# A searched order for all five engines, exchanged for another one: gated mix of a recurrent memory transformer and full attention

## The chip, the cores and the metric

One core of a Trainium2 chip runs the whole program. The metric is the device time of one execution in microseconds (us): 1329.91 as the median of three runs of the kernel before (1328.98 to 1330.77). The engines are named as in the profile: PE (TensorE matmul), PEld (TensorE weight load), DVE (VectorE), ACT (ScalarE), POOL (GpSimd) and SP (SyncE, which issues transfers).

## What is computed

Two attention models read the same input x (2048 tokens of 576 numbers, bfloat16) and are mixed by a gate per token.

```python
g = _sigmoid((x * gate_w).sum(-1, keepdims=True))
a = _A_ref(x, A_mem0, A_Wq, A_Wk, A_Wv, A_Wo, A_seg_len)   # recurrent, 64 segments
b = _B_ref(x, B_wqkv, B_wo)                                # full attention, 32 heads of 18
return g * a + (1 - g) * b
```

Model A walks through 64 segments of 32 tokens, one after the other. A segment's 8 memory rows and 32 tokens are projected to 32 heads of 128 for q, k and v, go through a masked softmax over 40 positions and an output projection; the first 8 rows of the result are the next segment's memory. Model B is plain softmax attention of 2048 by 2048 positions, with 32 heads of 18 numbers.

## The kernel before

**Work.** Model B runs as 32 groups of four heads and 512 queries, each with 16 blocks of 128 keys. One such block is a "visit": four matmuls in parallel give scores (L1066, tiles sb of three banks and sp of one), ACT takes the exponential of both (L1075 for 1536 columns, L1079 for 512), and PE multiplies the result with the values (L1089, ob). There are 512 visits. Model A's segment is a chain over several engines: PE projects q, k and v (L1438, pvv), DVE turns them (L1479) or copies them (L661), DVE or POOL puts the pieces in place (L1525 into qk, L1502 into v_sb), PE forms scores (L1539, L1547, psh), ACT the exponential (L1557), PE sums (L1568 or L1573, pss), DVE the reciprocal (L1585, rq), PE spreads it (L1593, prb), DVE scales (L1604, et), PE multiplies with v (L1615, pso), DVE or ACT copies out (ot), PE projects (L1320, acc), DVE adds (L1347 sum, L1648 obf), PE "folds" the memory rows (L1663 and L1670, pw) and DVE writes them into the next segment's input (L1679, ht). Only then can the next segment begin. The parts of model A that don't depend on the memory are computed ahead (L1157 and L1161, pv) and held in DRAM. At the start x is transposed (L724, evicted by L661 on DVE or L659 on ACT) and projected for model B (L871, L909); at the end the attention output is projected (L1834, L1838, tile po), combined with the gate on DVE (L1849), and stored by SP (L1859).

**Tile modes of PE.** A stage uses the array whole ("full", 128 rows by 128 columns), as four column strips ("col"), four row strips ("row", only the scores of model B), two row halves ("tall") or smaller squares ("quad").

**What sets the order.** `Plan` holds 8,581 operations with their dependences and with pools of numbered buffers (`tokens`): four shared PSUM banks "pb", one triple bank "sb", two "etb", and so on. `ORDER` is a table of five strings, one for each engine. A string holds differences between the numbers of successive operations, so the five lists together give the order on every engine, and also which engine does an operation that two can do. `run` takes the heads of the five lists in turn and replays them with stored durations; the replay decides which buffer of a pool an operation gets. `FULL` lists operations that are to use their whole-array form instead of the column form. Where the replay sees PE idle for long enough, `zeros` puts in a filler: a multiplication with zeros that adds nothing (L1037 in column strips, four matmuls each; L1043 whole).

```python
            at, queues[e] = 0, []
            for step in ORDER[e].split():
                at += int(step)
                queues[e].append(self.ops[at])
```

An engine works strictly through its list: a head that waits holds up all behind it, transfers included where that engine issues them.

Of the kernel before, what the change touches and what calls it, by code (L numbers as in the profile page):

```python
# [10 lines left out]
ACT = mybir.ActivationFunctionType  # L11
# [5 lines left out]
    "PE":  # L17
        "19 15 -5 -5 188 -24 -75 -39 -14 224 -234 75 -27 -14 116 -48 6 -50 32 3 3 -101 24 -14 82 12 6 -39 -13 -10 -14 "
        "91 -42 -9 42 33 -27 -36 3 -12 54 15 -27 39 -6 -15 -3 27 -21 -12 202 -166 6 164 -161 3 162 -5 4 -152 -6 163 "
        "-154 3 -9 159 7 -151 6 -9 158 -7 -139 -6 151 5 -147 9 137 5 -145 -3 147 7 -142 -3 142 7 -122 -21 147 -5 -139 "  # L20
        "143 -137 142 -145 9 135 7 -3 -121 -15 143 -134 -3 141 -5 -130 6 128 5 -130 3 126 11 -7 2293 -2420 138 2276 7 "
        "1 1 -2286 5 2273 1 -2275 2285 1 -2281 2271 11 -2283 2284 9 -2288 2289 -2290 2283 1 1 -2280 2281 5 4 1 -4 5 "
        "-2288 -5 2205 -2201 2202 88 -87 -2198 2199 1 3 -2204 5 2206 1 1 1 -2210 5 2206 3 -13 1 13 -2211 5 2207 -13 1 "
        "17 -2213 2209 -2204 2205 -2206 2216 -6 7 1 -2213 2225 -11 12 1 -21 1 -2208 2209 -2204 -1 2212 13 1 -11 1 1 1 "
        "-2213 2260 1 -47 52 -4 5 1 -5 -2259 -5 2273 -3 4 1 1 64 -2336 11 -7 2339 2 1 -2 3 3 -1 -2334 2336 -2337 2334 "
        "-73 1 1 -2258 2259 3 1 1 10 -9 -2261 -5 4 2272 -7 1 7 1 -2269 2262 10 1 -10 11 -2275 5 2271 9 -6 1 1 -2277 5 "
        "2273 4 -2278 2279 1 -2275 2319 7 -4 -2323 2321 7 -6 -2317 2311 8 6 -1 -2325 5 2322 4 -16 14 -2325 5 2319 -14 "
        "16 -17 -2305 5 -1 2363 7 -6 1 -2360 2366 -5 1 -39 -2324 5 2363 1 1 -2366 2338 -16 -2317 2319 -2320 2322 "
        "-2317 2331 -11 -2321 2334 -12 1 1 12 -2325 -7 2335 1 1 1 2 -2329 -1 2376 -4 3 -2 1 4 2 -2375 2374 -29 27 -26 "
        "3 -2350 2353 -5 -2343 2349 -5 3 -1 6 3 -2356 2354 -2349 2352 -2 3 3 -1 21 -22 -2355 5 2374 33 1 1 -33 34 -20 "  # L30
        "21 -2412 5 2374 -2375 2411 1 1 -24 25 -2409 2386 -13 37 -36 1 1 12 -2389 5 2387 1 1 1 -2391 2393 -2388 -1 "
        "2409 4 -3 7 14 -20 1 22 -2 1 2 4 -2434 2433 -2 1 -23 10 -9 1 -2412 2422 -6 -2411 2419 -3 2 21 -25 -2 1 -2414 "
        "5 2437 33 1 -32 33 1 1 -21 -2454 5 2437 36 1 1 -24 25 1 -2478 2454 -2449 2436 1 14 -13 1 -2440 5 2450 1 1 1 "
        "-2454 2456 -2443 -9 2494 1 2 -1 2 4 -2489 2486 1 1 -2489 2460 4 -1 4 -2462 2463 -7 1 4 -1 10 2 -2473 2472 -5 "
        "-2462 2470 -1 -4 -2466 2465 -1 27 -2484 2520 1 1 -36 37 1 -22 -14 -2491 7 2500 -2501 2487 37 1 1 1 -2522 "
        "2523 -38 13 -12 1 1 -2489 2501 -2496 -1 2500 1 1 1 -2496 2498 -2501 2524 4 -3 1 1 -2520 2525 -3 10 -9 10 -9 "
        "10 -2530 -5 2529 7 1 20 -25 -2 1 -2527 2555 -2550 2531 1 20 -18 -1 -2534 2567 -31 4 -2533 2531 45 -46 32 -30 "
        "45 1 1 -15 -2567 7 2576 -32 33 1 1 -2580 5 2543 1 1 13 -2559 2547 -2542 2557 1 1 1 -2561 2563 -2552 -7 2599 "
# [1863 lines left out]
```

## Time and profile before

| | before |
|---|---|
| median of three runs | 1329.91 us |
| the profiled execution: first to last instruction | 1326.1 us |
| around it (median less span) | 3.8 us |
| PE busy | 1291.3 us, 97% |
| ACT busy | 1113.3 us, 84% |
| DVE busy | 820.1 us, 62% |
| POOL busy | 611.5 us, 46% |

The page gives the profiled execution no time of its own beside its span. PE's busy time takes in the modelled ends of pipelined matmuls, so 97% doesn't mean that 3% alone is lost: gaps of some tenths of a microsecond are covered by it. They show in the starts of successive matmuls and in the idle time ahead of PEld.

### The profile page before, as it was taken

What the parts mean: (1) busy time and instruction counts of PE and PEld (TensorE: products, weight loads), DVE (VectorE), ACT (ScalarE), POOL (GpSimd) and SP (SyncE); (2) the same over time, 40 slices, a digit from 0 to 9 for tenths busy, and PEclk for the clock granted to TensorE, in tenths of its full rate; (3) what the DMA queues carried; (4) which work ended last, traced back from release to release, by engine and by line L of the source; (5) the groups of instructions that cost most, each with busy time, mean ns of one, the idle gap of its engine ahead of it and who ended that gap; (6) DMA issues with size and microseconds to landing.
All of it is one profiled execution on the core that took longest, in us unless ns stands there. A gap on an engine that the chain in (4) does not pass through costs nothing.

```text
span 1326.1 us, 73242 instructions
## 1 busy us (share of the span) xinstructions
PE 1291.3 (97%) x32951; PEld 694.1 (52%) x32951; DVE 820.1 (62%) x1821; ACT 1113.3 (84%) x1329; POOL 611.5 (46%) x1260
## 2 busy tenths in 40 slices
PE   8999899999999999999999999999999999999998
PEld 5555454555555545555555545555554445454445
DVE  5334466666666656666665665657665666666667
ACT  3688889988978888888888888888878999898895
POOL 4552475555444454343463454554345434644330
PEclk9999999999999999999999999999999999999999
DMA  8997420011201021200210111200113010201024
GB/s 254 290 309 233 134 64 22 29 47 37 64 18 44 26 57 30 53 17 23 58 48 17 35 50 32 68 24 26 38 35 81 16 32 11 52 21 34 19 79 149
DMA packets 110073, 88.63 MB, mean 67 GB/s; under 512 B 67271, under 2 KB 100375, under 8 KB 109759
## 3 DMA queue, kind: packets, MB, share of 16 engines
q1 hardware_dynamic: 92471, 50.92, 13.7%
q0 software_dynamic: 15152, 30.83, 7.7%
q8 instruction: 258, 4.23, 1.3%
q10 hardware_dynamic: 2136, 2.19, 0.6%
q14 instruction: 56, 0.46, 0.1%
HBM read 52.74 MB, written 31.12 MB: 63 GB/s over the span
## 4 chain that ended last, share of the span: by engine, by line
PE 83%; DVE 6%; ACT 4%; issue 3%; DMA 2%; POOL 1%; SPq 0%; DVEq 0%; ACTq 0%; POOLq 0%
PE pvv L1438 30%; PE sb L1066 11%; PE acc L1320 11%; PE ob L1089 8%; PE pv L1157 5%; ACT etb L1075 3%; PE pso L1615 3%; PE pq L871 3%; PE pv L1161 2%; PE psh L1547 2%; DVE v_sb L1502 2%; PE po L1834 1%; PE prb L1593 1%; PE pvb L909 1%; PE psh L1539 1%
## 5 line engine op out<-in xcount | busy, mean ns | idle before, releaser
L1075 ACT ACTIVATE etb<-sb 128x1536 bf16<-128x1536 f32 x512 | 743.4, 1452 | 121.5 <-PE sp L1066 83.0
L1079 ACT ACTIVATE etb<-sp 128x512 bf16<-128x512 f32 x512 | 305.2, 596 | 0.1
L1502 POOL COPY v_sb<-tm 32x512 bf16<-32x512 bf16 x344 | 217.1, 631 | 174.2 <-DVE tm L661 117.0
L1479 DVE STREAM_TRANSPOSE tf<-pvv 128x512 f32<-128x512 f32 x256 | 181.2, 714 | 171.0 <-PE pvv L1438 164.0
L1438 PEld LDWEIGHTS <-ht 128*32 128x32 bf16 (+1 forms) x7680 | 171.6, 94 | 218.6 <-issue 119.3
L1525 POOL CAST qk<-tf 128x512 bf16<-128x512 f32 x130 | 81.4, 628 | 297.3 <-DVE tf L1479 295.3
L1066 PE MATMUL sb<-qch,kch 32*128 32x512 bf16 x1536 | 200.6, 384 | 2.7 <-ACT etb L1075 1.2
L1089 PE MATMUL ob<-etb,vch 128*32 128x512 bf16 x2048 | 202.6, 382 | 0.3 <-DVE tq L1117 0.3
L1066 PE MATMUL sp<-qch,kch 32*128 32x512 bf16 x512 | 196.1, 383 | 0.1
L1438 PE MATMUL pvv<-wk_m,ht 128*32 128x512 bf16 x2048 | 165.0, 381 | 0.3
L1438 PE MATMUL pvv<-wq_m,ht 128*32 128x512 bf16 x2048 | 163.2, 381 | 1.3 <-DVE ht L1679 0.5
L1320 PE MATMUL acc<-wo,ot 128*32 128x288 bf16 (+1 forms) x6144 | 161.5, 247 | 1.5 <-DVE ot L661 0.5
L1438 PE MATMUL pvv<-wv_m,ht 128*32 128x512 bf16 x2048 | 154.6, 381 | 0.0
L1320 PEld LDWEIGHTS <-ot 128*32 128x32 bf16 x6144 | 112.4, 96 | 32.8 <-issue 10.7
L661 DVE CAST ot<-pso 128x320 bf16<-128x320 f32 x193 | 88.0, 484 | 49.5 <-PE pso L1615 46.7
L1066 PEld LDWEIGHTS <-kch 32*128 32x128 bf16 x2048 | 55.7, 91 | 114.4 <-issue 102.9
L661 DVE CAST tm<-pvv 128x512 bf16<-128x512 f32 x101 | 69.3, 687 | 42.3 <-PE pvv L1438 41.1
L1502 DVE COPY v_sb<-tm 32x512 bf16<-32x512 bf16 x168 | 75.0, 446 | 8.3 <-ACT tm L659 5.3
L1089 PEld LDWEIGHTS <-vch 128*32 128x32 bf16 x2048 | 54.5, 95 | 46.0 <-issue 29.9
L1604 DVE TENSOR_TENSOR et<-et,prb 128x320 bf16<-128x320 bf16 x128 | 61.9, 485 | 21.4 <-PE prb L1593 14.6
L1557 ACT ACTIVATE et<-psh 128x320 bf16<-128x320 f32 x128 | 55.9, 439 | 22.6 <-PE psh L1547 20.8
L1406 POOL COPY qk<-xl 128x128 bf16<-128x128 bf16 x256 | 65.6, 295 | 10.6 <-PE psh L1547 4.4
(161 smaller groups left out, 1839.4 us busy)
## 6 DMA issues: line engine op xcount, KB each, us to landing
xl<-qkd SPq DMA_DIRECT2D x16, 512.0 KB
qkd<-vl SPq DMA_DIRECT2D x37, 128.0 KB
wo<-in_A_Wo_dram POOLq DMA_DIRECT2D x8, 576.0 KB, 5.7
wq_m<-in_A_Wq_dram POOLq DMA_DIRECT2D x8, 512.0 KB, 5.5
vgd<-vt SPq DMA_DIRECT2D x32, 128.0 KB
wk_m<-in_A_Wk_dram POOLq DMA_DIRECT2D x8, 512.0 KB, 6.1
wv_m<-in_A_Wv_dram POOLq DMA_DIRECT2D x8, 512.0 KB, 6.6
v_sb<-vld SPq DMA_DIRECT2D x128, 32.0 KB
```

Of the source, the lines that this page charges most:

```text
L661: nc.vector.tensor_copy(out=out_of(), in_=in_of())
L1066: nc.tensor.matmul(sb[:, j, :] if j < 3 else sp[:, :], lhsT=kc[r, o:o + P], rhs=qt_[r, :], start=True, stop=True, tile_position=(32 * j, 0),)
L1075: nc.scalar.activation(out=etb[:, 0:3, :], in_=box["sb", gq, kb][:, :, :], func=ACT.Exp, scale=scale_b)
L1079: nc.scalar.activation(out=etb[:, 3, :], in_=box["sp", gq, kb][:, :], func=ACT.Exp, scale=scale_b)
L1089: nc.tensor.matmul(ob[32 * j:32 * j + 32, :], lhsT=vc[:, o + 32 * j:o + 32 * j + 32], rhs=etb[:, j, :], start=(kb == 0), stop=(kb == NKB - ...
L1157: nc.tensor.matmul(out_, lhsT=lw, rhs=rw, start=(c == 0), stop=(c == NF), skip_group_check=wide)
L1320: nc.tensor.matmul(acc[32 * q:32 * q + 32, :], lhsT=o[:, slot, t0:t0 + CT], rhs=wo[:, h, d:d + n], start=(first and s_ == (s_ % 2 if wide ...
L1406: nc.gpsimd.tensor_copy(out=opened["qk"][:, f, a, 0:16 * L].rearrange("p (u h t) -> p u h t", h=4, t=L)[:, :, :, CT:L], in_=xl[:, f, a, :, ...
L1438: nc.tensor.matmul(o, lhsT=ht[:, c, :], rhs=rw, start=start, stop=stop, tile_position=(r, 32 * j), skip_group_check=True,)
L1479: nc.vector.transpose(out=tf[:, :], in_=box["pvv", s, n][:, :])
L1502: move(out=opened["v_sb"][64 * (j // 2):64 * (j // 2) + CT, o:o + 512], in_=tm[32 * j:32 * j + CT, :],)
L1525: move(out=opened["qk"][:, hf, a, 0:16 * L].rearrange("p (k t) -> p k t", t=L)[:, :, 0:CT], in_=box["tf", s, "QK"[a] + str(hf)][:, :].rear ...
```

## The change

The five strings of `ORDER` and the list `FULL` are replaced by others; nothing else differs (the tables stand in brackets now, which moves all later line numbers up by 9). Operations, tiles, buffers and transfers are the same.

```diff
 ORDER = {
...
-    "POOL":
...
+    "POOL": (
+        "0 11 340 -320 80 -11 247 -333 323 -330 334 -236 244 -10 4 2 10 -284 -24 310 -4 -301 34 -50 323 -278 282 2 "
...
 FULL = (
-    2929, 2930, 2934, 2935, 2936, 2938, 3003, 3018, 3019, 3020, 3025, 3026, 3027, 3028, 3203, 3205, 3208, 3211,
...
+    2930, 2934, 2935, 2936, 2937, 2938, 3018, 3025, 3028, 3167, 3208, 3209, 3368, 3386, 3391, 3392, 3439, 3473,
...
```

Counted over the two programs: on PE the number of changes from one tile mode to another goes from 1582 to 1572, the fillers from 83 to 79. 503 operations change their engine. Most go both ways in like numbers; what is left over is 34 casts into qk and 34 pairs of copies into v_sb that go from POOL to DVE, and 94 transfer issues that go from SP to POOL (327 to 421 on POOL).

At the very start, ACT issues transfers and evicts a transposed block of x. The rows below are transfers of x (xn) and of model B's weights (wb), and copies of transposed blocks (xT from ptx). Before:

```order
L707 DMA xn_194<-in_A_x_dram 128x576
L707 DMA xn_197<-in_A_x_dram 128x576
L659 COPY xT_140<-ptx_175 128x5x128
L659 COPY xT_140<-ptx_208 128x5x128
L707 DMA xn_225<-in_A_x_dram 128x576
L769 DMA wb_141<-in_B_wqkv_dram 128x576
```

and now:

```order
L716 DMA xn_177<-in_A_x_dram 128x576
L778 DMA wb_141<-in_B_wqkv_dram 128x576 x2
L716 DMA xn_199<-in_A_x_dram 128x576
L778 DMA wb_141<-in_B_wqkv_dram 128x576
L668 COPY xT_140<-ptx_171 128x5x128
L716 DMA xn_219<-in_A_x_dram 128x576
```

ACT evicts one of the first four blocks of x instead of two, and issues ten transfers ahead of it where it issued seven ahead of the first.

In segment 20, DVE's list around the second half's reciprocal (rq), with copies of v (v_sb from tm), the copies out of pso, and the scaling of et1. Before:

```order
L661 CAST ot_1819<-pso_14960 128x320
L661 CAST ot_1819<-pso_14961 128x320
L1125 TENSOR_TENSOR tn_15035<-tq_14795,rtb_14874 128x512
L661 CAST tm_15045<-pvv_14868 128x512
L1585 RECIPROCAL rq_15072<-pss_15058 107x6
L1502 COPY v_sb_1812<-tm_15045 32x512 x2
L1604 TENSOR_TENSOR et1_1821<-et1_1821,prb_15092 128x320
```

and now:

```order
L670 CAST tm_14949<-pvv_14866 128x512
L1534 CAST qk_1816<-tf_14942 128x16x32
L670 CAST ot_1821<-pso_14963 128x320
L670 CAST ot_1821<-pso_14962 128x320
L1511 COPY v_sb_1814<-tm_14949 32x512 x2
L1594 RECIPROCAL rq_15058<-pss_15044 107x6
L1613 TENSOR_TENSOR et1_1823<-et1_1823,prb_15070 128x320
```

The two copies of v stood behind the reciprocal and stand ahead of it.

At the end, DVE's last combinations. The numbers of the po tiles rise in the order in which PE began them. Before:

```order
L1849 SCALAR_TENSOR_TENSOR wk_m_106<-po_42087,omg_70,wv_m_102 128x288
L1849 SCALAR_TENSOR_TENSOR wk_m_106<-po_42094,omg_70,wv_m_102 128x288
L1849 SCALAR_TENSOR_TENSOR wk_m_106<-po_42103,omg_70,wq_m_104 128x288
L1849 SCALAR_TENSOR_TENSOR wk_m_106<-po_42111,omg_70,wq_m_104 128x288
L1849 SCALAR_TENSOR_TENSOR wk_m_106<-po_42120,omg_70,wq_m_104 128x288
L1849 SCALAR_TENSOR_TENSOR wk_m_106<-po_42029,omg_70,wq_m_104 128x288
```

and now:

```order
L1858 SCALAR_TENSOR_TENSOR wk_m_106<-po_42076,omg_70,wv_m_102 128x288
L1858 SCALAR_TENSOR_TENSOR wk_m_106<-po_42083,omg_70,wv_m_102 128x288
L1858 SCALAR_TENSOR_TENSOR wk_m_106<-po_42091,omg_70,wv_m_102 128x288
L1858 SCALAR_TENSOR_TENSOR wk_m_106<-po_42099,omg_70,wv_m_102 128x288
L1858 SCALAR_TENSOR_TENSOR wk_m_106<-po_42107,omg_70,wq_m_104 128x288
L1858 SCALAR_TENSOR_TENSOR wk_m_106<-po_42115,omg_70,wq_m_104 128x288
```

An older tile was combined last, behind the newest; now the newest is combined last. SP stores a block of rows as soon as both its halves are combined, in the matching order: the store behind that older tile was SP's last, and now the store of the newest one is.

## Rows read from the trace of the kernel before

**Rows 1.** The page's first and fourth part: busy time, and the chain by engine.

```profile
PE 1291.3 (97%) x32951; PEld 694.1 (52%) x32951; DVE 820.1 (62%) x1821; ACT 1113.3 (84%) x1329; POOL 611.5 (46%) x1260
PE 83%; DVE 6%; ACT 4%; issue 3%; DMA 2%; POOL 1%; SPq 0%; DVEq 0%; ACTq 0%; POOLq 0%
```

**Rows 2.** Timeline of PE from 603 us: start us, us, what, count.

```profile
603.33 0.39 PE L1066 MATMUL sp<-qch,kch 32*128 32x512 bf16 x1
603.65 0.40 PE L1438 MATMUL pvv<-wv_m,ht 128*32 128x512 bf16 x4
603.87 0.39 PE L1089 MATMUL ob<-etb,vch 128*32 128x512 bf16 x4
604.09 0.61 PE L1438 MATMUL pvv<-wq_m,ht 128*32 128x512 bf16 x8
```

**Rows 3.** Groups by line, PE's fillers: count, busy us, mean ns, idle before.

```profile
L1037 PE MATMUL ob<-ident,nil 128*32 128x512 bf16 x328 | 30.6, 380 | 0.5 <-issue 0.5
```

**Rows 4.** Waits of the weight loads: us in total, times, longest.

```profile
PEld L1663 <- DVE obf L1648: 22.5, 57, 0.7
PEld L1593 <- DVE rq L1585: 13.5, 37, 0.9
PEld L1320 <- DVE ot L661: 6.8, 25, 0.6
PEld L1573 <- ACT et L1557: 6.4, 27, 0.6
PEld L1438 <- DVE ht L1679: 6.0, 17, 0.4
```

**Rows 5.** The page's groups: ACT's two exponentials of a visit.

```profile
L1075 ACT ACTIVATE etb<-sb 128x1536 bf16<-128x1536 f32 x512 | 743.4, 1452 | 121.5 <-PE sp L1066 83.0
L1079 ACT ACTIVATE etb<-sp 128x512 bf16<-128x512 f32 x512 | 305.2, 596 | 0.1
```

**Rows 6.** Timelines of PE and ACT in segment 20.

```profile
516.25 0.60 PE L1438 MATMUL pvv<-wk_m,ht 128*32 128x512 bf16 x8
516.68 0.82 PE L1037 MATMUL ob<-ident,nil 128*32 128x512 bf16 x12
517.55 0.39 PE L1066 MATMUL sb<-qch,kch 32*128 32x512 bf16 x3
...
516.05 1.45 ACT L1075 ACTIVATE etb<-sb 128x1536 bf16<-128x1536 f32 x1 [0.30 <-PE sp L1066]
```

**Rows 7.** Timeline of the first 14 us, all engines.

```profile
3.55 0.61 PE L724 MATMUL ptx<-ident,xn 128*128 128x128 bf16 x4 [3.55 <-POOL vt L681]
...
6.35 1.29 ACT L659 COPY xT<-ptx 128x640 bf16<-128x640 bf16 x2 [4.33 <-PE ptx L725]
...
7.12 0.33 ACTq L707 DMA_DIRECT2D xn<-in_A_x_dram  x1
...
7.64 0.16 PEld L871 LDWEIGHTS <-wb 128*128 128x128 bf16 x2 [1.30 <-DMA wb<-in_B_wqkv_dram]
7.69 5.76 PE L871 MATMUL pq<-xT,wb 128*128 128x512 bf16 x15 [1.08 <-ACT xT L659]
...
8.03 0.89 ACTq L707 DMA_DIRECT2D xn<-in_A_x_dram  x2
```

**Rows 8.** Timeline of the end, all engines; SP's stores.

```profile
1316.37 6.92 SPq L1859 DMA_DIRECT2D out_dram<-wk_m  x12
...
1320.78 1.50 DVE L1849 SCALAR_TENSOR_TENSOR wk_m<-po,omg,wq_m 128x288 bf16<-128x288 f32 x3
...
1321.02 0.29 PE L1838 MATMUL po<-wq_t,stage 128*128 128x288 bf16 x1
```

**Rows 9.** Copies into v_sb: duration min/median/max, first and last start.

```profile
L1502 POOL COPY v_sb<-tm x344: 599/607/1077, 142.9 to 1289.2; 32x512 bf16<-32x512 bf16 x172
L1502 DVE COPY v_sb<-tm x168: 239/391/741, 148.6 to 1290.8; 32x512 bf16<-32x512 bf16 x168
```

**Rows 10.** Groups by line on DVE: the copies that the change moves.

```profile
L1502 DVE COPY v_sb<-tm 32x512 bf16<-32x512 bf16 x168 | 75.0, 446 | 8.3 <-ACT tm L659 5.3
L1525 DVE CAST qk<-tf 128x512 bf16<-128x512 f32 x126 | 57.7, 465 | 2.8
```

**Rows 11.** Transfers of keys issued by POOL, and who waited for such loads.

```profile
L986 POOL DMA_DIRECT2D kch<-ktd x44: 505/505/657, 175.7 to 1158.2; - x44
...
PEld L1066: 0.5, 2
```

More of the change, by code (lines that the diff above doesn't have):

```diff
@@ L16 @@
 ORDER = {
[158 rows of a table removed]
-    "DVE":
[52 rows of a table removed]
-    "ACT":
[41 rows of a table removed]
-    "POOL":
[38 rows of a table removed]
[160 rows of a table added]
+    ),
+    "DVE": (
[56 rows of a table added]
+    ),
+    "ACT": (
[41 rows of a table added]
+    ),
+    "POOL": (
[23 rows of a table added]
+    ),
[13 rows of a table added]
+    ),
 }
 FULL = (
[5 rows of a table removed]
[5 rows of a table added]
 )
```

589 rows, old and new, of tables (FULL, ORDER) are left out of this document.

## Prediction

> **What bounds the kernel now.** I read the page's busy shares first, then the chain that ended last, then PE's timeline, the waits of the weight loads, and last the two ends of the span. PE is busy 97% of the span and carries 83% of the chain [rows 1]; no other engine is near it except ACT with 84% of its time. So the end is set by PE's work plus the moments in which PE has nothing ready. The busy share hides these moments, so I took them from the starts of matmuls. In column strips a group of four starts every 0.22 us (603.65, 603.87, 604.09), but from the row strips of the scores to the first column group it takes 0.32 (603.33 to 603.65) [rows 2]: a change of tile mode costs 0.10 us. Each of the 4,501 PE pieces other than fillers, laid end to end at the pitch that its kind shows where the next one follows without a gap, with 0.104 for each change of mode, gives 1220.3 us. PE starts at 3.55 [rows 7] and its last matmul ends at 1321.3, 4.8 before the end of the span [rows 8]. The rest, 1326.1 - 3.55 - 4.8 - 1220.3 = 97 us, are moments in which the next piece wasn't ready. The 83 fillers stand in such moments; 82 of them are the 328 matmuls of [rows 3], 30.6 us.
>
> What PE waits for there: 57 folds wait for DVE's sum (22.5 us), 37 spreads for the reciprocal, 25 projections for copies out of pso, 27 sums for the exponential, 17 first projections of a segment for DVE's ht [rows 4]. And the scores wait for ACT, whose two exponentials of a visit take 1.45 + 0.60 = 2.05 us [rows 5]. In segment 20 three fillers run from 516.68, and the scores start at 517.55, just as the exponential that began at 516.05 ends (517.50) [rows 6].
>
> **The change part by part.** No operation goes or comes, so the sum has four terms: mode changes, the moments in which PE waits, the start and the end. I add them to the profiled execution's span of 1326.1; the median of the runs is 3.8 above it, and I carry this over.
>
> *Mode changes.* 1582 become 1572, fillers counted or not ten fewer: -10 x 0.104 = -1.0 us. The choice between whole array and strips differs in two or three pieces, worth less than 0.1.
>
> *Moments of waiting.* I can't read from the order how long PE waits, but I can count how much PE work stands between the two ends of each link, with the pitches above, and compare it with what the link needs. The need of each kind is what its fastest twentieth took in this trace, start to start less the first piece's own pitch. Where the work is shorter than the need, the difference is a shortfall. The count for before agrees with the trace: 50 folds are short (57 waits), 37 spreads (37 waits), 22 sums (27), 21 first projections (17) [rows 4], and all shortfalls together are 88.8 us against the 97 found above. The same count in the new order gives 85.5. The largest part is the bank of a visit's fourth score tile, which is free only after both exponentials: 25.1 us in 113 places become 19.0 in 107. Segment 20 shows how: three more projections stand ahead of the scores where the three fillers were, but two fillers appear behind the next pso product. Scaling gains 0.8 and the first projection behind ht 0.9. Copies out of pso on DVE lose 1.4 (23 places become 32), folds 0.6, the next output sums 0.6, the start of the final outputs of a group 0.8. All kinds that fall come to -9.7, all that rise to +6.4. I take the sum, -3.3; the ends are kept for the range.
>
> *Start.* The first projection waits for the four transposed blocks and the weights. Before, ACT evicts the last block after its two copies from 6.35, and PE starts at 7.69; the weights arrived at 7.64 as well, so nothing earlier is to be had [rows 7]. Now ACT's one copy stands behind ten transfers, the fifteenth that ACT and SP issue together. Before, the fifteenth was issued at 7.12 and took 0.33, so the copy would start at 7.45 and, at 0.65 a copy (1.29 for two), let PE start at about 8.15: +0.5. If ACT's own count decides, the tenth of its transfers was issued at 8.03 and took 0.44 (two in 0.89) [rows 7], and PE starts at 9.1: +1.4. The lower end is 0. I take +0.5, since transfers were issued when earlier ones had landed, whichever engine issued them.
>
> *End.* PE's last matmul ends at 1321.3 and the last store is issued until 1323.3 (1316.37 + 6.92), 2.0 later, because SP works off its list with the store of an older tile behind all others. Now the last store needs only the newest combination: 0.05 + 0.5 (1.50 for three) + 0.45 for the issue is 1.0 behind PE [rows 8]: -1.0. The lists in between leave slack: eleven stores behind the last load need 5 us, and 19 final products of 0.61 stand behind the last ob. If SP is still backed up, it is 0.
>
> *Engine moves.* POOL loses 102 copies and gets 94 transfer issues of 0.5 us [rows 11], so it stays about as busy. DVE gets 68 copies of 0.446 and 34 casts of 0.465 [rows 10], +46 us on an engine that is 62% busy. I cost this at nothing, since PE work covers DVE in all but the short places, which are counted; what it costs without that cover is the third rival. Loads that move to POOL are issued long before their use: PE's scores waited 0.5 us in all for such transfers [rows 11].
>
> Sum: -1.0 - 3.3 + 0.5 - 1.0 = -4.8. Span 1321.3, median 1325.1 us.
>
> **The rivals.**
>
> *Nothing measurable.* The gains of the count are taken back by its losses, since ACT's exponentials pass at 2.05 us whatever PE does between them, and the start costs its upper end: -1.0 + 0 + 1.4 - 1.0 = -0.6, 1329.3 us. For it: ACT is 84% busy, and the largest term is ACT's. Against it: ACT still waited 83 us for scores [rows 5], so PE, not ACT, is late more often.
>
> *Much faster.* The kinds that rise stand in places where PE waits anyway for something else, and only the falls count: -1.0 - 9.7 + 0.5 - 1.0 = -11.2, 1318.7 us. For it: shortfalls overlap, as the fillers of segment 20 cover two links. Against it: that is as true of the falls.
>
> *Slower: DVE's queue.* In 107 places, 83 before, a copy into v_sb or qk stands on DVE directly ahead of a reciprocal, a scaling or a copy out of pso; segment 20 is one. Each holds its follower, and with it PE, by up to its own mean of 0.446 to 0.465 [rows 10]. All 24 uncovered cost 24 x 0.455 = +10.9, with the -4.8 it is +6.1: 1336.0 us. It decides from 11 of the 24 uncovered, and shows as slower from 17. For it: a copy on DVE takes 0.239 at best and 0.741 at worst, on POOL 0.599 to 1.077 [rows 9], so copies are held up while both engines run, and now more of them run on DVE. Against it: POOL loses as many copies. The Trainium skill ("SBUF — State Buffer", section "SBUF: two separate sides") says that the two engines share a pair of ports which one instruction holds to its end while the other engine is blocked, and that descriptors of transfers issued on GpSimd are held up by this too. The spread of the copies agrees with it. By that rule the 94 added issues would land later and the added copies would run nearer 0.74 than 0.45, on the side of this rival; the wait of 0.5 us for such loads doesn't bear out that half of it.
>
> **How the numbers follow.** A difference of 0.2%, 2.7 us, is about what a measurement of this kernel can tell from none, so faster is below 1327.2 and slower above 1332.6. Forecast (about 1321 to 1327): 0.46. Much faster: 0.16. Nothing measurable: 0.24. DVE's queue: 0.14. Faster 0.62, same 0.24, slower 0.14. The ends of the sum itself are -1.0 - 9.7 + 0 - 1.0 = -11.7 (1318.2) and -1.0 + 6.4 + 1.4 + 0 = +6.8 (1336.7). The range 1319 to 1331 leaves out half of the much faster case and most of the slower one, under 0.2 together.
>
> **What would show it.** Mode changes: the starts of [rows 2] keep their 0.10. Waiting: fillers 316 matmuls instead of 328, the waits of folds still near 57, ACT's idle time ahead of L1075 for PE (83.0) a few us lower. Start: the first projection at 8.0 to 8.3. End: the last store about 1.0 behind the last matmul's end instead of 2.0. The prediction is wrong if waits of weight loads for et, rq or ot on DVE grow by more than 5 us together, or if the copies into v_sb on DVE rise well above 0.45 in the mean.

## The result: 1.0% slower, and the profile after

The changed kernel takes 1341.24 us (1340.33 to 1343.28, 4 runs), before 1329.45 beside it: 11.8 us more by the medians. The ratio that is used below is 1.0102 [1.0082, 1.0122], which is 13.6 us of before. The forecast was 1325.1, with 1331 as the upper end. The profiled execution took 1343.28 us, span 1341.5; 2.0 above the median, so a sum over its trace comes out a little too large. Lines behind L320 stand 9 further down than before.

The page's first, fourth and fifth part: busy time, the chain by engine, and the groups of ACT's first exponential and of DVE's copies into v_sb:

```profile
PE 1296.7 (97%) x32944; PEld 696.7 (52%) x32944; DVE 842.6 (63%) x1928; ACT 1112.6 (83%) x1327; POOL 600.8 (45%) x1249
PE 78%; DVE 9%; ACT 4%; DMA 4%; issue 3%; SPq 1%; POOL 1%; DVEq 0%; ACTq 0%; POOLq 0%
...
L1084 ACT ACTIVATE etb<-sb 128x1536 bf16<-128x1536 f32 x512 | 743.5, 1452 | 132.6 <-PE sp L1075 87.5
L1511 DVE COPY v_sb<-tm 32x512 bf16<-32x512 bf16 x236 | 96.5, 409 | 11.2 <-ACT tm L668 7.1
```

And the groups by line: PE's fillers, DVE's casts, and POOL's transfers of keys (busy us, mean ns, idle before):

```profile
L1046 PE MATMUL ob<-ident,nil 128*32 128x512 bf16 x316 | 30.7, 380 | 0.7 <-issue 0.7
L1534 DVE CAST qk<-tf 128x512 bf16<-128x512 f32 x160 | 70.9, 454 | 2.5
L995 POOL DMA_DIRECT2D kch<-ktd x68 | 34.7, 518 | 7.3 <-PE sp L1075 5.2 <-issue 1.4 <-DMA qkd<-vl 0.5
```

Against [rows 1] PE's share of the chain falls from 83 to 78%, DMA's rises from 2 to 4 and DVE's from 6 to 9. ACT's idle time ahead of its first exponential for PE was to fall from 83.0 [rows 5]; it rose to 87.5. A copy into v_sb takes DVE 409 ns instead of 446 and a cast 454 instead of 465 [rows 10], so longer copies are not the reason; an issue of POOL takes 0.52 us, as in [rows 11]. The fillers are 316 matmuls for 328 [rows 3]. The waits of PE's weight loads, against [rows 4]:

```profile
PEld L1672 <- DVE obf L1657: 24.7, 57, 0.7
PEld L1602 <- DVE rq L1594: 18.4, 47, 0.8
PEld L1329 <- DVE ot L670: 7.5, 24, 1.1
PEld L1447 <- DVE ht L1688: 5.9, 19, 0.4
PEld L1582 <- ACT et L1566: 5.8, 26, 0.4
PEld L1624 <- DVE et L1613: 4.3, 10, 0.8
```

The last of these, in before:

```profile
PEld L1615 <- DVE et L1604: 2.6, 9, 0.6
```

The reciprocal's wait grew most, from 13.5 to 18.4 us. With et (2.6 to 4.3) and ot (6.8 to 7.5) the three grew by 7.3 us together: the prediction had named more than 5 as a sign that it is wrong. The rest of the loss stands in four places of the timeline.

First the start: the queues of ACT and SP and PE's first projection, where [rows 7] had 7.69:

```profile
5.26 2.97 ACTq L778 DMA_DIRECT2D wb<-in_B_wqkv_dram  x2
6.04 2.62 SPq L778 DMA_DIRECT2D wb<-in_B_wqkv_dram  x4
8.60 0.33 ACTq L716 DMA_DIRECT2D xn<-in_A_x_dram  x1
9.71 0.34 ACTq L778 DMA_DIRECT2D wb<-in_B_wqkv_dram  x1
10.09 0.69 ACT L668 COPY xT<-ptx 128x640 bf16<-128x640 bf16 x1 [8.06 <-DMA wb<-in_B_wqkv_dram]
...
10.83 2.29 PE L880 MATMUL pq<-xT,wb 128*128 128x512 bf16 x5 [4.10 <-ACT xT L668]
```

ACT's copy stands behind the transfers of its queue. The row of 2.97 us is two issues with a wait for a landing between them (a single one mostly takes 0.33 to 0.45), and the last goes at 9.71, not at 7.12. It is the fifteenth transfer in the planned order, but on the chip SP had issued its four of 6.04 to 8.66 by then, so it was the nineteenth to go (ten of ACT, nine of SP). Five traces with this start begin the projection between 9.92 and 10.83.

Second, what DVE's copies of model A's products (tile vl) wait for between 105 and 150 us:

```profile
DVE vl L670 <- DMA qkd<-vl: 10.1, 4, 4.1
DVE vl L670 <- DMA vld<-vl: 4.6, 1, 4.6
```

And the timeline of POOL there, when it gets on:

```profile
120.90 0.40 POOL L1247 MEMSET ht<- 128x160 bf16 x2 [24.82 <-DMA vgd<-vt]
127.08 0.77 POOL L1265 DMA_DIRECT2D wo<-in_A_Wo_dram  x1 [0.39 <-issue]
```

A wait of DVE for a DMA *out of* vl is a wait for a staging buffer: the next product can't be copied until the store of an older one has landed. The two come to 14.7 us. In the kernel before there is one such row, of 4.8 us; it stands here with POOL's timeline:

```profile
DVE vl L661 <- DMA vld<-vl: 4.8, 3, 3.2
```
```profile
113.11 0.68 POOL L1246 MEMSET obf<- 128x704 bf16 x1 [8.86 <-DMA ktd<-xn]
...
119.98 0.77 POOL L1256 DMA_DIRECT2D wo<-in_A_Wo_dram  x1 [6.19 <-DVE et L1273]
```

POOL opens the memory of the output weights (wo, 576 KB a load) when the last projection is stored: 113 us before, 121 now.

Third, the middle, POOL and then DVE:

```profile
633.63 2.02 POOL L995 DMA_DIRECT2D otd<-stage  x4 [2.82 <-issue]
635.64 2.00 POOL L995 DMA_DIRECT2D qch<-qtd  x4
637.63 0.62 POOL L1534 CAST qk<-tf 128x512 bf16<-128x512 f32 x1
...
638.29 1.32 DVE L1488 STREAM_TRANSPOSE tf<-pvv 128x512 f32<-128x512 f32 x2 [2.73 <-POOL qk L1534]
```

Eight transfers keep POOL for 4.0 us, its cast stands behind them, DVE waits 2.73 us for the buffer that the cast reads, and PE's next piece starts 1.62 us later than it would without a wait.

Fourth the end, SP's stores and PE's last matmul, for [rows 8]:

```profile
1330.43 7.97 SPq L1868 DMA_DIRECT2D out_dram<-wk_m  x11
...
1337.16 0.29 PE L1847 MATMUL po<-wq_t,stage 128*128 128x288 bf16 x1
```

The last store is issued by 1338.40, 0.95 behind the end of PE's last matmul (1337.45): here the change won, as forecast.

To see where time goes I laid each kernel's PE pieces end to end as in the prediction and took the waiting beyond that, against before at equal PE work, from one profiled execution each (us; the columns are before's time there). The rows below the first are the experiments of the next section:

```
                        15     69    106    154    210    450    697    end
after                  2.6    3.3    4.9    8.6   10.9   12.1   16.8   17.2
before_first          -0.3    2.0    2.0   -1.0   -1.0    0.0    4.6    7.8
after_first            1.6    2.8    4.2    6.2    9.7   13.5   16.1   22.0
after_first_pinned     3.4    4.1    6.0    7.4   10.5   10.7   10.4   13.1
before_to_50          -1.0    3.1    4.6    7.2   12.3   13.0   18.3   19.3
before_to_104         -0.2    0.9    0.9    1.3    3.6    5.2   10.0   11.2
xT_copy_early         -0.1    0.6    2.8    6.2    7.2    9.2   15.8   19.8
xT_copy_pinned         0.0    1.1    1.9    5.3    7.7    8.5   13.2   14.7
readback_late          2.9    3.6    5.7    8.2    9.9   11.0   15.3   17.2
front_mended          -1.2    0.8    1.3    9.7   11.4   12.1   16.6   17.4
front_mended_2        -0.5   -0.1    4.7    4.4   11.6   12.6   17.0   19.0
mid_transfers         -0.9    1.0    2.9    4.5    6.7    7.6    8.6   11.5
all_mended             0.3    1.4    3.2    2.4    9.0    9.7   11.5   14.9
recips_first          -1.0    0.5    2.1    5.1    7.7    9.3   11.0   21.5
before_first_mended   -1.0    0.6    0.6   -2.3   -2.3   -1.0    1.9   10.1
transfers_back         1.6    1.7    7.4    8.5    9.8   11.7   12.9   21.1
copies_back            1.1    2.1    6.6   15.1   17.9   21.6   42.2   52.9
before_xl_first        0.5    3.5    3.5    1.1    1.7    1.4    2.1    1.7
before_recips_first   -0.7    0.7    0.7   -1.3   -1.2   -0.8    0.8    1.8
```

Between executions of the same order a column differs by up to about 3.5 us where transfers are dense (45 to 160 us): before_xl_first has 3.5 at 69 and 106 us, where its order is still that of before, and from 69 to 106 us front_mended_2 rises by 4.8 and front_mended by 0.5 with one and the same order there. So a ratio settles the sum, and a column only says where. A part of the spread is PE's clock. In 15 of the 20 profiled executions it falls to 1.2 GHz (granted clock 0.50) for one or more stretches while PE still works; before has none, the changed kernel one (48.7 to 52.1 us). Most begin in or behind a wait of PE: at 153.6 us in front_mended, in one of 6.4 us, and at 763.8 in transfers_back, behind one of 2.4. In the changed kernel's stretch five matmuls of a projection (pq) take 2.01 us, where readback_late has 1.24 at 2.4 GHz. By that clock a stretch costs at most half its length, and that is in the columns.

### The profile page after: what moved, and what is told of

The parts are those of the page before. It is cut to its first block, busy times and chain, and to the rows that moved or that the text cites. A ratio compares the mean times of both kernels' runs of the same rounds, so it can differ in the third digit from the quotient of the medians.

```text
span 1341.5 us, 73118 instructions
## 1 busy us (share of the span) xinstructions
PE 1296.7 (97%) x32944; PEld 696.7 (52%) x32944; DVE 842.6 (63%) x1928; ACT 1112.6 (83%) x1327; POOL 600.8 (45%) x1249
## 4 chain that ended last, share of the span: by engine, by line
PE 78%; DVE 9%; ACT 4%; DMA 4%; issue 3%; SPq 1%; POOL 1%; DVEq 0%; ACTq 0%; POOLq 0%
PE pvv L1447 28%; PE sb L1075 10%; PE acc L1329 10%; PE ob L1098 7%; PE pv L1166 3%; PE pq L880 3%; ACT etb L1084 3%; PE pso L1624 3%; PE pv L1170 2%; DVE v_sb L1511 2%; PE psh L1556 2%; PE prb L1602 1%; PE po L1843 1%; DVE et L1613 1%; DVE tm L670 1%
## 5 line engine op out<-in xcount | busy, mean ns | idle before, releaser
L1084 ACT ACTIVATE etb<-sb 128x1536 bf16<-128x1536 f32 x512 | 743.5, 1452 | 132.6 <-PE sp L1075 87.5
L1447 PEld LDWEIGHTS <-ht 128*32 128x32 bf16 (+1 forms) x7680 | 175.9, 94 | 214.8 <-issue 115.4
L1511 POOL COPY v_sb<-tm 32x512 bf16<-32x512 bf16 x276 | 172.4, 624 | 199.0 <-DVE tm L670 138.6
L1534 POOL CAST qk<-tf 128x512 bf16<-128x512 f32 x96 | 62.2, 648 | 260.5 <-DVE tf L1488 255.9
L1447 PE MATMUL pvv<-wv_m,ht 128*32 128x512 bf16 x2048 | 158.1, 381 | 1.6 <-DVE tf L1488 1.5
L1511 DVE COPY v_sb<-tm 32x512 bf16<-32x512 bf16 x236 | 96.5, 409 | 11.2 <-ACT tm L668 7.1
```

The costliest lines, as they stand in the source:

```text
L1084: nc.scalar.activation(out=etb[:, 0:3, :], in_=box["sb", gq, kb][:, :, :], func=ACT.Exp, scale=scale_b)
L1447: nc.tensor.matmul(o, lhsT=ht[:, c, :], rhs=rw, start=start, stop=stop, tile_position=(r, 32 * j), skip_group_check=True,)
L1511: move(out=opened["v_sb"][64 * (j // 2):64 * (j // 2) + CT, o:o + 512], in_=tm[32 * j:32 * j + CT, :],)
L1534: move(out=opened["qk"][:, hf, a, 0:16 * L].rearrange("p (k t) -> p k t", t=L)[:, :, 0:CT], in_=box["tf", s, "QK"[a] + str(hf)][:, :].rear ...
```

## The experiments

Orders are tables of numbers, so edits are told as moves of named instructions in one engine's list. One thing moves along with most edits: the replay decides anew which of the four banks "pb" a tile gets. Of its 1,957 choices some 500 to 1,800 come out otherwise in most kernels below than in the kernel that they start from; in readback_late and mid_transfers (from xT_copy_pinned) none do. What another choice of banks costs by itself was not tested.

**Which stretch.** Two kernels joined from the orders of both: up to an instant the instructions that one kernel has placed by then, in its order, then all others in the other's order.

```
+ first = ops placed by 212 us in before (in after)
  for e in engines:
-     queue[e] = after[e]
+     queue[e] = [o in before[e] if o in first] + [o in after[e] if not in first]   # and the reverse
```

> Before's order on all five engines for the instructions that before has placed by about 212 us of its execution, then the changed order for all that is left. Theory (the time is lost in the stretch in which the weights are loaded and model A's products are made and stored, through waits on transfers and on buffers that stores give back): the profile of the changed kernel has lost 10.9 us on before by 208 us, of which about 2 is a stretch of half clock at 48.7 to 52.1 us that may be of that execution alone; so 1341.2 - 9 = about 1332, range 1329.5 to 1334. Rival (the engine moves, 68 more copies on VectorE and 94 transfers moved to GpSimd, cost evenly all along): the first 16% of the time carries 16% of the 11.8 us, so about 1339.

Measured: 1.0045 [1.0029, 1.0062], 6.0 us above before. Between the two theories' numbers, nearer the first: the changed order also loses behind 212 us.

> The opposite half: the changed order for what the changed kernel has placed by about 212 us, then before's order. Theory: before's time and the 9 us lost in the first stretch, about 1338.5, range 1336 to 1341. Rival (the cost is spread evenly by the engine moves): about 1331.5. If the two halves' differences from before do not add up to 11.8 us, the two stretches interact.

Measured: 1.0158 [1.0135, 1.0181]. Neither; worse than the whole change. Its planner had placed 95 groups of fillers, 380 matmuls, instead of 83 or 79. So I fixed the fillers, each ahead of the same piece of PE as in its own kernel:

```
-                w = self.zeros(op, est, mode)
+                w = self.pinned(op)      # FILL[op.seq]: the fillers that this kernel has ahead of op
```

> after_first (the changed order to 212 us, before's behind it) with the fillers of each kernel pinned in its own part, 83 groups where after_first's planner placed 95. Theory (the loss by 212 us is about 9 us and before's order loses nothing more behind it; what after_first lost there came with the fillers): 1.0065 to 1.008 of before. Rival (before's order behind 212 us fits only the state that its own first part leaves): 1.012 to 1.016 as after_first.

Measured: 1.0075 [1.0062, 1.0089], 10.0 us: the theory. In the table it loses 10.5 by 210 us, then nothing up to 697, and 2.7 behind that, where PE waits at 1300 us and then has 1.2 GHz for 3.4 us. With before_first, 10.0 + 6.0 = 16 for 13.6 ± 2.7 of the whole: the two stretches add up within their intervals, the larger part in the first 212 us.

**The start.**

```
+ ("ACT", "xe3", "ahead of", "wb23"),
```

> The changed kernel, with ScalarE's first copy of transposed x (xe3) moved ahead of the transfers wb23, wb21, x9 and wb11 in ScalarE's list. Theory: this copy waits from 5.3 to 10.1 us behind transfers that wait for a free transfer slot, and TensorE's first projection waits for it; it would start at about 8 us as before, the whole about 2.6 us earlier: 1338.6, range 1337.8 to 1340. Rival: the four transfers, later by the copy's 0.7 us, or the weights that land at their own pace, hold the projections in its place and the time stays within 0.7 us of 1341.2.

Measured: 1.0114 [1.0098, 1.0131]: the rival's number, nothing gained. Yet its first column is 2.7 us lower than the changed kernel's: the start was mended, and the loss came back behind 550 us, with 46 more fillers.

> As xT_copy_early (ScalarE's first copy of transposed x ahead of four transfers), but with exactly the 316 filler matmuls of the changed kernel, each ahead of the same instruction; in xT_copy_early the planner, whose own estimate of the waits had moved, placed 362. Theory (the start's 2.8 us were won, and 46 more fillers and what they shift lost them again): about 2.8 us under the changed kernel, 1.008 of before. Rival (the start's gain is given back at the next wait on transfers, whatever the fillers): 1.010 to 1.0115 as before.

Measured: 1.0065 [1.0043, 1.0087]: the theory. ACT's copy and PE's first projection, and the fillers of xT_copy_early and of this kernel:

```profile
5.34 0.69 ACT L703 COPY xT<-ptx 128x640 bf16<-128x640 bf16 x1 [3.31 <-PE ptx L769]
...
7.48 2.29 PE L915 MATMUL pq<-xT,wb 128*128 128x512 bf16 x5 [0.83 <-DVE xT L705]
```
```profile
L1059 PE MATMUL ob<-ident,nil 128*32 128x512 bf16 x360 | 33.8, 380 | 0.0
L1065 PE MATMUL ob<-ident,nil 128*128 128x512 bf16 x2 | 0.6, 379 | 0.0
```
```profile
L1081 PE MATMUL ob<-ident,nil 128*32 128x512 bf16 x316 | 30.4, 380 | 0.0
```

The projection starts at 7.48 instead of 10.83, and the gain lasts to the end of the table (14.7 for 17.2). The two kernels have the same order and differ in fillers, and with them in 1,274 choices of banks: 1.0114 against 1.0065, and 5.1 us in the table.

**The stores of model A's products.**

```
+ ("SP", "lw0", "behind", "ls0.1.6"), ("SP", "fs0", "behind", "lw0"),
```

> The changed kernel, with two transfers of SyncE, lw0 (reads model A's v back from DRAM, and so waits for eight stores to land) and fs0, moved from ahead of the eight stores ls0.1.0 to ls0.1.7 to behind them. Theory: these stores, held from 129.2 to 134.6 us, give back the three staging buffers for which VectorE's copies and then TensorE wait; the waits of 1.86 us at 137.3 and 2.9 us at 142.7 go, 1336.5, range 1335.5 to 1339. Rival: the stores' landing is slow by the four output-weight loads of 576 KB that are under way beside them (landing 132 to 147 us), so the buffers come as late as now: within 1 us of 1341.2.

Measured: 1.0075 [1.0058, 1.0091]. In its trace the wait at 137 us is gone, but DVE waits 5.3 us for a store of vl up to 146.7, and by 154 us only 0.4 is won in the table, less than executions differ by. The ratio lies between; the trace is for the rival.

```
+ ("ACT", "xe3", "ahead of", "wb23"),  lw0 and fs0 as above,
+ ("POOL", "lh1", "ahead of", "wo4"),  ("DVE", marks of wo6, wo4, wo0, wo1, "ahead of", "mkwo3"),
```

> The changed kernel with its own fillers pinned and three places of the first 160 us mended at once: xe3 ahead of the four transfers on ScalarE; lw0 and fs0 behind the eight stores ls0.1.x on SyncE; and four of the eight output-weight loads (wo6, wo4, wo0, wo1, 576 KB each) held until VectorE has copied all eight products of that group, where in the changed kernel they land beside the stores. Theory (the stores' landing, slowed by the loads beside them, holds the staging buffers): the waits at about 137 and 143 us, 4.8 us together, go, and 2.8 us at the start, so 1.010 - 0.0055 = 1.0045 of before (1336). Rival (the loads then land too late for the output product at 165 us, or the landing is slow by itself): the waits come back there, and only the start's 2.8 us stay, 1.008.

Measured: 1.0103 [1.0079, 1.0126], the rival's side, though at another place than it named. Both waits are gone, and one larger stands at 152.6 us. POOL, and PE's weight load:

```profile
141.24 2.98 POOL L1307 DMA_DIRECT2D wo<-in_A_Wo_dram  x4 [12.37 <-DVE wo L846]
...
158.54 1.00 POOL L1457 COPY qk<-xl 128x128 bf16<-128x128 bf16 x4 [8.44 <-DMA xl<-qkd]
...
159.11 0.34 PEld L1598 LDWEIGHTS <-qk 128*32 128x32 bf16 x31 [6.42 <-POOL qk L1457]
```

The four loads that had been held were issued together, and the read-back xl landed behind them.

```
  hold wo0, wo6, wo1 only;  + ("POOL", "pl0", "ahead of", "wo0"), ("SP", "ll0", "ahead of", "fs0"),
```

> front_mended with two corrections: only three output-weight loads are held (wo0, wo6, wo1), and they are issued behind GpSimd's copy of the projected products that SyncE reads back from DRAM (xl), with that read-back issued ahead of fs0; in front_mended four held loads were issued at 141.2 us, 3 us ahead of this read-back, and TensorE waited 6.4 us for it at 152.6 us. Theory (who lands first decides, the sum of bytes is the same): the waits at 137, 143 and 152 us are all gone or under 1 us, 1.0103 - 0.005 = about 1.005 of before. Rival (the stretch is bound by what has to be stored, loaded and read back in it, so one of the three waits stays whichever goes first): 1.008 to 1.0105.

Measured: 1.0106 [1.0088, 1.0123]: the rival. At 154 us the table has 4.4, at 210 11.6. In all_mended, which has the same edit, PE now waits for the weights that were put off:

```profile
163.59 0.78 PE L1365 MATMUL acc<-wo,ot 128*32 128x144 bf16 x32 [1.14 <-DMA wo<-in_A_Wo_dram]
165.11 0.43 PE L1365 MATMUL acc<-wo,ot 128*32 128x144 bf16 x16 [0.74 <-DMA wo<-in_A_Wo_dram]
```

So in these three runs whichever of stores, read-back and loads was put last was waited for. Whether the lateness is made earlier was asked by joining the orders at two other instants, with pinned fillers.

> Before's order for what before has placed by 50 us, the changed order behind it, fillers pinned. Theory (beyond the start's 2.8 us, the loss of the first stretch is made by the order between 50 and 104 us, which issues the projections' last stores late and so opens the memory for the output weights late): as xT_copy_pinned, with the waits at 113 to 143 us in the trace, 1.0065 to 1.009 of before. Rival (it was set before 50 us, by the transfers lost at the start): those waits are gone, 1.004 to 1.0055, as before_first.

Measured: 1.0091 [1.0074, 1.0108]; the waits at 114 to 137 us are there, and DVE waits 10.4 us for stores: the theory.

> Before's order for what before has placed by 104 us, the changed order behind it, with its read-back lw0 and fs0 ahead of the eight stores ls0.1.x and its order of the output-weight loads; fillers pinned. Theory (the late projections do it): GpSimd's wait for the last projection store ends at about 113 to 115 us, the waits at 137 and 143 us shrink to under 1 us together, 1.0045 to 1.006 of before. Rival (the read-back ahead of the stores does it by itself): at least 3 us of waits stay between 130 and 150 us, 1.0065 to 1.0085.

Measured: 1.0066 [1.0048, 1.0083]. When POOL gets on, and what DVE's copies wait for:

```profile
113.25 0.69 POOL L1272 MEMSET obf<- 128x704 bf16 x1 [8.69 <-DMA ktd<-xn]
```
```profile
DVE vl L687 <- DMA qkd<-vl: 4.4, 2, 3.9
DVE vl L687 <- DMA vld<-vl: 1.8, 1, 1.8
```

Both theories have a part. The opening is at 113 us again, the waits for stores fall from 14.7 to 6.2 us, and of the loss by 154 us 1.3 is left where before_to_50 has 7.2 (at most 3.4 of that are its two stretches at 1.2 GHz). But 2.8 us of PE's waits at 132 and 138 remain, nearly the rival's 3, with the read-back and the loads of the changed order; before_first, without these, has -1.0. The ratio lies at the edge of the two forecasts.

**Engines.** First all 242 copies and casts that change between DVE and POOL, then all 113 transfers that change between SP and POOL, were put back on before's engine, in the changed order's place. The 148 operations that change between DVE and ACT were left as they are; no run tests them.

> The changed kernel with its fillers pinned, and all 242 copies and casts that change sides between VectorE and GpSimd put back on the engine that before gives them, at the same place of the planned order. Theory (GpSimd's transfers and the order of the loads cost the time after 210 us, about 5 us): GpSimd gets 0.3 us more for each of the copies that come back, the time stays or rises, 1.010 to 1.013. Rival (VectorE's queue: the copies that the change gave it stand ahead of the reciprocal, whose start after its product is 227 ns on average where before has 157): the broadcast's waits fall by about 2 us, and the fold's, 1.006 to 1.008.

Measured: 1.0306 [1.0272, 1.0341]; slower, far more than I expected. PE's waits for POOL in this kernel, which were 2.5 for v_sb and 0.8 for the cast in the changed one:

```profile
PEld L1641 <- POOL v_sb L1528: 12.6, 26, 1.4
PEld L1573 <- POOL qk L1551: 4.8, 7, 2.8
```

That is 14 us more, of 35.7 more in the table. PE also waits 5.2 us up to 147.8, where a copy of DVE has waited 5.89 for a store of vl to land. And PE's clock is lower: 34 us at 1.2 GHz in seven stretches, at most 17 us of the 52.9; over the five runs the time goes from 1365.99 us at a mean granted clock of 0.996 to 1378.92 at 0.988. So the copies can't be put on POOL at these places of the order without losing more; that they cost nothing on DVE isn't shown by this.

> The changed kernel with its fillers pinned, and all 113 transfers that change sides between SyncE and GpSimd put back on the engine that before gives them, at the same place of the planned order. Theory (GpSimd's issues, 0.5 us each, stand ahead of its casts and copies): the wait of 1.6 us at 637 us, behind eight issues, goes, and others of its kind, 3 to 5 us in all, 1.006 to 1.008. Rival (VectorE's queue, or the order itself): no change, 1.009 to 1.011.

Measured: 1.0132 [1.0107, 1.0156], worse than both forecasts. The wait at 637 us is gone, and between 450 and 697 us the table rises by 1.2 instead of 4.7, as the theory said. Behind 697 it loses 8.2, for instance 2.4 at 761 us, where a fold waits for DVE's obf. The 5.7 between 69 and 106 us don't come from the edit: the first of the 113 transfers stands at about 120 us in the plan, and up to there the order is the changed kernel's, which loses 1.6.

> As xT_copy_pinned, and of the 113 transfers that change sides between SyncE and GpSimd only the 37 that the plan places between about 430 and 740 us put back on the engine that before gives them. Theory (GpSimd's issues stand ahead of its casts and copies in this stretch; transfers_back gained about 3.5 us there by its trace, and lost more at 74 to 80 us and after 750 us): xT_copy_pinned's 1.0065 less 3.5 us, 1.004 of before; in the trace the stalls that the changed kernel adds between 450 and 715 us fall from 4.7 to about 1.2 us. Rival (the gain was that execution's, or is given back at the next wait): 1.006 to 1.008.

Measured: 1.0088 [1.0065, 1.0111]. In the table the stretch from 450 to 697 us costs 1.0 instead of 4.7: the theory, at its place. It is no accident of one execution: the nine kernels that have the changed order and its transfers in this stretch lose 4.3 to 6.6 there (copies_back apart), the five that have before's engines for these transfers 1.0 to 2.9. At 1159 us a new wait of 2.25 for a cast on POOL takes part of it back; all_mended and recips_first, with the same 37 transfers, have it too. The total is on the rival's side: against xT_copy_pinned's 1.0065 it shows no gain. Its six runs spread from 1337.32 us to 1347.62, the slowest at a mean granted clock of 0.991.

> front_mended_2 and mid_transfers together: the changed kernel with its fillers pinned, the start, the stretch to 160 us and the 37 transfers of the middle mended. Theory (three places, about 2.8, 4 and 3.5 us, which add up): 1341 - 10.5, 1.000 to 1.004 of before. Rival (what is mended comes back as later waits): 1.006 and above.

Measured: 1.0099 [1.0082, 1.0116]: the rival. Of its 14.9 us 6.6 come between 154 and 210, where the loads of wo are late and PE has 1.2 GHz from 166.5 to 170.0.

**VectorE's queue.** In the changed kernel's trace the reciprocal of 32 softmaxes (of 128) starts more than 0.3 us behind its product, fifteen of them directly behind a copy into v_sb; in before's 18 and eight.

```
+ ("DVE", "rc0.15", "ahead of", "qc0.15"), ("DVE", "rc0.16", "ahead of", "qd0.16"), ...   # fourteen
```

> mid_transfers, and on VectorE fourteen of the softmax reciprocals moved ahead of the one or two v copies (0.7 to 0.9 us) that stand directly before them in the changed order. Theory (VectorE's queue: copies that the change moved there stand ahead of the reciprocal, whose broadcast then waits; the waits at these fourteen places are 5.0 us in the changed kernel's trace): the waits of the broadcast fall from about 10 to 7 us or less in the trace, 2 to 4 us under mid_transfers, 1.003 to 1.007 of before. Rival (each copy put off makes the output product wait instead): no change against mid_transfers, 1.0075 to 1.0095.

Measured: 1.0122 [1.0107, 1.0138]: neither, slower than mid_transfers by 4.5 ± 3.7 us. What PE's products of the two kinds waited for, in mid_transfers and then here, and DVE at one of the fourteen places here:

```profile
L1652 PE MATMUL pso<-et,v_sb 64*128 64x40 bf16 x2048 | 49.2, 178 | 7.3 <-DVE et L1641 3.5 <-POOL qk L1443 0.4 <-ACT etb L1116 0.4
L1630 PE MATMUL prb<-ident,rq 107*32 107x107 bf16 x1536 | 42.1, 214 | 3.6 <-DVE rq L1622 2.7
```
```profile
L1666 PE MATMUL pso<-et,v_sb 64*128 64x40 bf16 x2048 | 49.5, 178 | 11.8 <-DVE et L1655 8.7 <-ACT etb L1130 0.4 <-POOL v_sb L1553 0.3
L1644 PE MATMUL prb<-ident,rq 107*32 107x107 bf16 x1536 | 41.7, 213 | 1.0 <-DVE rq L1636 0.3
```
```profile
453.32 0.20 DVE L1636 RECIPROCAL rq<-pss 107x6 bf16<-107x6 f32 x1 [0.35 <-PE pss L1624]
453.54 0.91 DVE L1553 COPY v_sb<-tm 32x512 bf16<-32x512 bf16 x2
454.48 0.72 DVE L1530 STREAM_TRANSPOSE tf<-pvv 128x512 f32<-128x512 f32 x1
455.23 0.49 DVE L1655 TENSOR_TENSOR et<-et,prb 128x320 bf16<-128x320 bf16 x1
```

The spread (prb) hardly waits for DVE now, 0.3 for 2.7 us. But at this place the copy and a transpose run between the reciprocal and the scaling (et), and over all segments pso waits 8.7 for et instead of 3.5. In mid_transfers the copy ran while DVE would have waited for the spread. These rows balance to 2.8 us more, of 10.0 in the table; PE's clock has three stretches at 1.2 GHz for one, at most 3.4 us of it, and the rest isn't explained.

> before_first (before's order to 212 us, the changed order behind it) with pinned fillers, the 37 transfers of the middle back on the engine that before gives them, and the fourteen reciprocals moved ahead of the copies. Theory (what the changed order loses behind 212 us is those two things: 3.7 and about 3 us of the 7.8 that its trace loses): 1.000 to 1.002 of before. Rival (what is mended comes back as later waits): 1.003 to 1.0055.

Measured: 1.0059 [1.0045, 1.0073]: the rival; no better than before_first. At 697 us its trace is 2.7 better than that of before_first, and behind it it loses 8.2 instead of 3.2. recips_first loses much there too, 10.5 where mid_transfers loses 2.9, so the reciprocals' moves are the likely cause; no run has them alone.

**Before itself.**

> The kernel before, its fillers pinned, with three output-weight loads on GpSimd (wo5, wo6, wo1) moved behind its copy of the read-back xl, which in before waits 4.0 us for that read-back to land beside them; TensorE waits 2.1 us at 147.9 us and 0.9 us at 152.3 us there. A candidate that would beat both kernels. Theory (the same contention as in the changed kernel): 2 to 3 us less than before, 0.998 to 0.9985. Rival (the output product at 157 us then waits for the loads that were put off): 0.9995 to 1.001.

Measured: 0.9992 [0.9980, 1.0003]. The wait at 147.9 us is gone, but the total can't be told from no change.

> before_xl_first, and on VectorE eight of before's own reciprocals moved ahead of the copies or casts that stand directly before them; the broadcasts' waits at these places are 3.7 us in before's trace. A candidate to beat both kernels. Theory (VectorE's queue): 1.5 to 2.5 us less than before_xl_first's 0.9992, 0.997 to 0.9982. Rival (the waits are given back at the product that needs the copies): 0.999 to 1.0005.

Measured: 1.0022 [1.0010, 1.0035]: slower, above both forecasts. Its twelve runs go from 1329.50 to 1334.65 us, and the profiled one is the quickest, so no trace shows what the others lose. No version was shown to beat before.

## Why the prediction was wrong, point by point

- *Mode changes and end.* The end came as said (0.95 for 1.0 behind PE). The fillers fell to 316 as counted, and the folds still wait 57 times. These terms are small, and nothing speaks against the first.
- *The start, +0.5.* Mis-sized: it cost 3.1 us in the profiled execution (10.83 for 7.69), 2.2 to 3.1 over five traces, and xT_copy_pinned took it back by one move. I took the time at which before issued its fifteenth transfer as given. But the transfer ahead of ACT's copy, the fifteenth of the plan, was the nineteenth to be issued, at 9.71 instead of 7.12: SP went on issuing while ACT's queue waited for landings. The upper end, 1.4, rested on before's times as well.
- *Moments of waiting, -3.3.* This is the step that failed. Without the start (2.6) the table has PE wait 14.6 us longer, not 3.3 shorter. The term counted how much PE work stands between two pieces linked by one instruction of DVE or ACT. It didn't count buffers that come free only when a store has landed, transfers that wait in SP's queue for a landing, or a read-back behind them. Between 15 and 154 us the changed kernel loses 6.0 (after_first and after_first_pinned, with the same order there, 4.6 and 4.0), at most 1.7 of it the stretch at 1.2 GHz; between 105 and 150 DVE waits 14.7 us for stores instead of 4.8. before_to_50 and before_to_104 show that most of it goes with the order from 50 to 104 us; that of 104 to 154 makes about 2 in the table (1.3 for -1.0), no more than executions differ by. From 450 to 697 us it loses 4.7 more, 3.7 of it with the 37 transfers that POOL now issues ahead of its casts, which the term didn't count either. And what it did count rose instead of falling: by the waits of [rows 4] the folds' grew by 2.2 us and the reciprocal's by 4.9, which it didn't name among its losses. Why the reciprocal's grew stays open.
- *Engine moves, nothing.* Wrong in its reason. "Loads that move to POOL are issued long before their use" holds, PE hardly waits for them; what waits is POOL's own cast behind the issues. By the table 37 transfers cost 3.7 us between 450 and 697 us. The timed total gained nothing without them: mid_transfers gave it back elsewhere, 2.25 us of it at 1159.
- *The rival with DVE's queue, 0.14.* It had the sign, and by its 1336.0 us it came nearest of the four cases; the waits for et, rq and ot grew by 7.3 us. But a copy got no longer (409 ns for 446), and no run won time by easing this wait: taking the copies off DVE cost 27 us more (1.0306 for 1.0102), and moving the reciprocals ahead 4.5 (1.0122 for 1.0088). So the queue has a part of the loss, of a size that is not known, and the wait is not a price that was saved by moving it. The Trainium skill ("SBUF — State Buffer", section "SBUF: two separate sides") has DVE and POOL hold each other up on a shared port; copies on DVE got shorter in the mean with more of them there, 446 to 409 ns, so the mean gives that no support.
- *What stays open.* About 3 us that the changed order loses between 210 and 500 us and what before_first_mended loses behind 697 weren't taken apart. Nor was the part of the banks. Why TensorE ran at 1.2 GHz from 48.7 to 52.1 us in the changed kernel's profiled execution (granted clock 0.74 over 50 to 54 us) is known in part: 1.0 us earlier it had ended the gate's 80 small matmuls (from 45.52 us). In four more traces the clock falls within 1.1 us of the end of these; readback_late, with the same matmuls at 45.83, has 1.00 there, so they don't always bring it.

## What to carry to other kernels

A reordering is priced by every queue, not by the busiest engine's links: list what each buffer waits for to come free, stores' landings included, and what stands behind each issue on the engine that issues it. Where a kernel is tuned by order, a local mend often moves the wait; take the next consumer's wait into the sum before believing the gain. Hold fixed what a planner adds by itself (here fillers, and better the choice of banks too) before comparing two orders. And read the granted clock beside each trace before a difference of a few microseconds is put down to an edit: where two orders are the same, their traces show what execution alone does.

## What was not expected of the hardware

Forty-six more filler matmuls, 34.4 us of PE's time for 30.4, placed where the planner saw waits, went with 5.1 us more in the table (the choice of banks differs too): PE's waits seem not to have lain where they had been planned. And the same 23 matmul records are missing from nine of the traces (the page then counts PE x32921 beside PEld x32944), so pieces are better counted by the weight loads.
